# Second half of a weight load dropped: the last 64 channels of the first layer, rounded part and rest in one tile

## The chip, the cores and the metric

The kernel runs on one core of a Trainium2 chip. The metric is the device time of one execution in microseconds. A change is compared by the median of several runs; three runs of the kernel before gave 1145.97, 1151.23 and 1152.69 us, a median of 1151.23 us.

## What is computed

Tokens of width 192 pass a causal convolution of 7 taps whose weights are a softmax, and then a mixture of experts: 4 groups of 4 experts, one expert for each token, two matrix products with a relu between them.

```
x = attn_out.reshape(B * S, D)              # 23040 tokens, D = 192
g_idx = argmax(x @ w_group); e_idx = argmax(xg @ w_expert[g])
h  = np.maximum(xg[mask_e] @ w1[g, e], 0.0) # w1: 192 x 1024
ye = h @ w2[g, e]                           # w2: 1024 x 192
out[tok_idx] = combined[:, None] * ye       # softmax weights of group and expert
```

## The kernel before, in words

**Routing.** The tokens are cut into 18 units of 4, 8 or 12 blocks of 120 tokens. For each unit TensorE does the convolution (L452), transposes (L475, L483) and the router's logits (L495, L497); VectorE turns the logits into an expert and a place for every token (L539 to L626); GpSimd scatters token numbers into a table in memory (`idtab`, L645). The convolved tokens are written to memory from the queue of ScalarE (`xcd<-xc`, L570); the tile `xc` that is written has three buffers. The buffer `rowi` of the scatter's rows has two, so VectorE's instruction that writes `rowi` for unit 2 (L626) waits until the scatter of unit 0 has landed.

**Visits.** An expert is visited several times, each visit with 256 tokens. GpSimd gathers the tokens by their numbers (`xg<-xcd`, L717), TensorE transposes them (L750 to L754), and the products follow. Early visits run beside the routing (until some 450 us). Then come pairs of visits that share their weights (512 tokens, L786 to L805), and last a tail of 9 visits of 256 tokens and 9 of 128 in turn (L817 to L839 and L852 to L878), each with weights of its own. All engines run their instructions in order; a scheduler has set that order from the program.

**Products in three parts.** Each float32 operand is split into a rounded part and a rest, and a product is the sum of rounded x rounded, rest x rounded and rounded x rest. For the first 128 of the 192 channels these are three matmuls (`ah`, `al` with the tokens' `xa`). For the last 64 channels two matmuls do it over 128 partitions: the 64 weight rows lie twice in the tile `rb` (two loads of 256 KB, L667 and L668, one into each half). `bh` holds their rounded part twice and `bl` their rest twice, while the tokens' tile `xb` holds the rounded part in one half and the rest in the other. So `bh` x `xb` and `bl` x `xb` together give all four products.

**Weights of a visit** (`weights`, L652 on): five loads from SyncE's queue, in this text `ra` (512 KB, L666), the two halves of `rb`, and two loads of second-layer weights `rc` (384 KB each, L670). `ra` and `rb` come from one ring of three buffers named `raw`, or every second time in the tail from a spare tile named `xin`. ScalarE makes the rounded parts (L682, L690, L697) and VectorE the rests (L683, L691, L698); in the tail GpSimd makes `bl` (L691).

**Tokens of a visit** (`turn`, L739 on): the transposed tokens lie in one PSUM bank. ScalarE copies the rounded part, VectorE writes the rest, first for `xa`, then for `xb`. In the trace these four steps follow each other, the second ScalarE copy starting only after the first VectorE step. From the 17th visit on up to the tail the last 64 channels of the two tiles are packed and done in two halves of 128 tokens. A pair of visits keeps its `xb` in a tile named `xc`.

**Early order.** The first weights are loaded before the table is cleared (L269, L272): `clear_table` is issued on SyncE's queue behind the first visit's loads, and the first scatter waits for it.

Of the kernel before, what the change touches and what calls it, by code (L numbers as in the profile page):

```python
# [20 lines left out]
P = 128  # L21
# [3 lines left out]
SLOT = 256  # L25
# [11 lines left out]
def conv_moe_kernel(  # L37
# [614 lines left out]
    def weights(r1, r2, eng=None, spare=False):  # L652
        eng = eng or {}
        HF = NF // 2
        if spare:

            rab = pa2.tile([P, UB, D], F32, name="xin").rearrange("p b d -> p (b d)")
            ra, rb = (rab[:, k * F:(k + 1) * F] for k in range(2))
            rcc = pa2.tile([P, UB, XE], F32, name="xc", bufs=3).rearrange("p b d -> p (b d)")
            rc = [rcc[:, k * HF * D:(k + 1) * HF * D].rearrange("p (f d) -> p f d", d=D) for k in range(2)]  # L660
        else:
            ra, rb = (wraw.tile([P, F], F32, name="raw") for _ in range(2))
            rc = [wraw.tile([P, HF, D], F32, name="rawc") for _ in range(2)]
        npin[0] += 1
        hold = tc.keep_in_program_order if NPIN[0] < npin[0] <= NPIN[1] else lambda ins: ins
        hold(nc.sync.dma_start(out=ra, in_=w1f[bass.ds(r1, P), :]))  # L666
        hold(nc.sync.dma_start(out=rb[0:D2], in_=w1f[bass.ds(r1 + P, D2), :]))  # L667
        hold(nc.sync.dma_start(out=rb[D2:P], in_=w1f[bass.ds(r1 + P, D2), :]))  # L668
        for k in range(2):
            hold(nc.sync.dma_start(  # L670
                out=rc[k], in_=w2f[bass.ds(r2 + k * HF * P, HF * P), :].rearrange("(f p) d -> p f d", p=P),
            ))
        W = {}

        def split(k):
            if k == 0:
                W["ah"] = ah = wsp.tile([P, F], F32R, name="ah")
                W["al"] = al = wsp.tile([P, F], F32R, name="al")
                if 8 in eng:
                    nc.gpsimd.tensor_copy(out=ah, in_=ra)  # L680
                else:
                    pin(PINA, nc.scalar.activation(out=ah, in_=ra, func=AF.Copy))  # L682
                eng.get(k, nc.vector).tensor_tensor(out=al, in0=ra, in1=ah.bitcast(F32), op=ALU.subtract)  # L683
            elif k == 1:
                W["bh"] = bh = wsp.tile([P, F], F32R, name="bh")
                W["bl"] = bl = wsp.tile([P, F], F32R, name="bl")
                if 9 in eng:
                    nc.gpsimd.tensor_copy(out=bh, in_=rb)
                else:
                    pin(PINB, nc.scalar.activation(out=bh, in_=rb, func=AF.Copy))  # L690
                eng.get(k, nc.vector).tensor_tensor(out=bl, in0=rb, in1=bh.bitcast(F32), op=ALU.subtract)  # L691
            else:
                if k == 2:
                    W["cw"] = wsp.tile([P, NF, 2, D], F32R, name="cw")
                cw = W["cw"]
                fs = slice((k - 2) * HF, (k - 1) * HF)
                pin(PINW, nc.scalar.activation(out=cw[:, fs, 0, :], in_=rc[k - 2], func=AF.Copy))  # L697
                eng.get(k, nc.vector).tensor_tensor(  # L698
                    out=cw[:, fs, 1, :], in0=rc[k - 2], in1=cw[:, fs, 0, :].bitcast(F32), op=ALU.subtract,
                )  # L700
# [38 lines left out]
    def turn(xs, n=2, packed=False, into=None, single=False):  # L739
        if into is None:  # L740
            px = pm.tile([P, 512], F32, name="pm")
            xa = ff.tile([P, 2, SLOT], F32R, name="xa")
            xb = ff.tile([P, SLOT], F32R, name="xb")
            xh, xl = xa[:, 0], xa[:, 1]
        else:
            px = pm.tile([P, 512], F32, name="pm") if single else ph.tile([P, 2, SLOT], F32, name="ph").rearrange("p a b -> p (a b)")
            xh, xl, xb = into
        w = n * P
        for t in range(n):
            nc.tensor.transpose(px[:, t * P:(t + 1) * P], xs[t][:, 1:1 + P], ident)  # L750
            if not packed:
                nc.tensor.transpose(px[0:D2, SLOT + t * P:SLOT + (t + 1) * P], xs[t][:, 1 + P:XW], ident)
        if packed:
            nc.tensor.transpose(px[:, SLOT:SLOT + P], xs[0][:, 1 + P:XE], ident)  # L754
        nc.scalar.activation(out=xh[:, 0:w], in_=px[:, 0:w], func=AF.Copy)
        nc.vector.tensor_tensor(out=xl[:, 0:w], in0=px[:, 0:w], in1=xh[:, 0:w].bitcast(F32), op=ALU.subtract)
        if packed:
            for t in range(2):
                hi, lo = slice(t * D2, (t + 1) * D2), slice((1 - t) * D2, (2 - t) * D2)
                cs = slice(t * P, (t + 1) * P)  # L760
                pb = px[hi, SLOT:SLOT + P]
                nc.scalar.activation(out=xb[hi, cs], in_=pb, func=AF.Copy)
                nc.vector.tensor_tensor(out=xb[lo, cs], in0=pb, in1=xb[hi, cs].bitcast(F32), op=ALU.subtract)
            return None if into else (xa, xb)
        pb = px[0:D2, SLOT:SLOT + w]
        nc.scalar.activation(out=xb[0:D2, 0:w], in_=pb, func=AF.Copy)
        nc.vector.tensor_tensor(out=xb[D2:P, 0:w], in0=pb, in1=xb[0:D2, 0:w].bitcast(F32), op=ALU.subtract)  # L767
        return xa, xb

    def pair_room():  # L770
        hi = ff.tile([P, 2, SLOT], F32R, name="xa").rearrange("p a b -> p (a b)")
        lo = pa.tile([P, 512], F32, name="lts", bufs=2).bitcast(F32R)
        xb = pa2.tile([P, UB, XE], F32, name="xc", bufs=3).rearrange("p b d -> p (b d)")[:, 0:512].bitcast(F32R)
        return hi, lo, xb

    def turn_half(X, k, xs, single=False):
        cs = slice(k * SLOT, (k + 1) * SLOT)
        turn(xs, 2, True, [x[:, cs] for x in X], single)

    def hidden_pair(W, X, f):  # L780
        xh, xl, xb = X
        hp = ph.tile([P, 2, SLOT], F32, name="ph")
        fs = slice(f * P, (f + 1) * P)
        ops = (("ah", xh), ("al", xh), ("ah", xl), ("bh", xb), ("bl", xb))
        for i, (wgt, xx) in enumerate(ops):
            nc.tensor.matmul(  # L786
                out=hp.rearrange("p a b -> p (a b)"), lhsT=W[wgt][:, fs], rhs=xx, start=i == 0, stop=i == len(ops) - 1)
# [20 lines left out]

    def hidden(W, X, f2, hook=lambda: None):
        xa, xb = X  # L810
        ah, al, bh, bl = (W[n] for n in ("ah", "al", "bh", "bl"))
        hp = ph.tile([P, 2, SLOT], F32, name="ph")
        for j in range(2):
            fs = slice((2 * f2 + j) * P, (2 * f2 + j + 1) * P)
            ops = ((ah, xa[:, 0]), (al, xa[:, 0]), (ah, xa[:, 1]), (bh, xb), (bl, xb))
            for i, (wgt, xx) in enumerate(ops):
                nc.tensor.matmul(out=hp[:, j], lhsT=wgt[:, fs], rhs=xx, start=i == 0, stop=i == len(ops) - 1)  # L817
            if j == 0:
                hook()
# [25 lines left out]
    def hidden_small(W, X, h):  # L845
        xa, xb = X
        hp = ph.tile([P, 512], F32, name="ph")
        fs = slice(h * 512, (h + 1) * 512)
        xh, xl, xb = xa[:, 0, 0:P], xa[:, 1, 0:P], xb[:, 0:P]
        ops = ((xh, "ah"), (xh, "al"), (xl, "ah"), (xb, "bh"), (xb, "bl"))  # L850
        for i, (xx, wgt) in enumerate(ops):
            nc.tensor.matmul(out=hp, lhsT=xx, rhs=W[wgt][:, fs], start=i == 0, stop=i == len(ops) - 1)  # L852
        hr = pa.tile([P, 512], F32, name="lts", bufs=2)
        nc.scalar.activation(out=hr, in_=hp, func=AF.Relu)
        return hr
# [633 lines left out]
```

## Time and profile before

| | value |
|---|---|
| median of three runs | 1151.23 us |
| time of the profiled execution | 1152.26 us |
| its span, first to last instruction | 1150.4 us |
| mean granted TensorE clock | 0.977 |
| TensorE busy | 1072.8 us, 93% |
| VectorE, ScalarE, GpSimd busy | 752.4, 644.1, 523.5 us |
| moved by DMA | 166.08 MB, 144 GB/s in the mean |

Busy shares are means over stages with different limits, so the stages are read apart in windows of the span. A wait is given as the idle time of an engine ahead of an instruction and the event that ended it. An instruction's start and length stand in the timeline; on one engine the next one may start some tens of ns before the last one's end. The chain is followed back from the last instruction.

### The profile page before, as it was taken

Reading aid. Unit: us, or ns where it says so; the run is one execution under the profiler, and the core shown is the slowest. Engines: PE = TensorE matmul, PEld = TensorE weight load, DVE = VectorE, ACT = ScalarE, POOL = GpSimd, SP = SyncE. Lnnn points to the kernel's source line nnn. Section 1 sums busy time; section 2 is a strip of 40 time slices with the busy share of each in tenths; the row PEclk is TensorE's granted clock in tenths of the full one; section 3 lists DMA queues with packets and bytes.
Section 4 is the critical chain, followed back from the end, with each engine's and each line's share of the span. In section 5 each row is a group of like instructions: output and inputs, shape, how many; then the busy total and the mean of one; then the engine's idle time right before and its main releaser. Section 6 shows DMA issues by size and latency. Waiting matters only on the chain.

```text
span 1150.4 us, 20931 instructions
## 1 busy us (share of the span) xinstructions
PE 1072.8 (93%) x7124; PEld 971.1 (84%) x7124; DVE 752.4 (65%) x1671; ACT 644.1 (56%) x1362; POOL 523.5 (46%) x611
## 2 busy tenths in 40 slices
PE   6565999998999998999999999999999999999996
PEld 4444788987989998889899999999999988989986
DVE  3465878987778756576565555655556665687874
ACT  5445657765657554454455445554545555677873
POOL 3004143333334454554545454545445554487773
PEclk9878989999999999999999999999999999999998
DMA  8767688999566432332253223322333435499970
GB/s 185 186 158 228 160 222 215 252 234 216 156 155 164 122 106 85 116 112 67 83 137 113 72 76 99 113 74 73 103 101 106 133 92 157 116 257 257 252 201 19
DMA packets 143167, 166.08 MB, mean 144 GB/s; under 512 B 18946, under 2 KB 124397, under 8 KB 143054
## 3 DMA queue, kind: packets, MB, share of 16 engines
q1 hardware_dynamic: 100974, 111.04, 36.4%
q0 software_dynamic: 18752, 35.85, 10.5%
q10 hardware_dynamic: 23328, 17.80, 6.6%
q8 instruction: 57, 0.93, 0.3%
q14 instruction: 56, 0.46, 0.1%
HBM read 129.43 MB, written 36.58 MB: 144 GB/s over the span
## 4 chain that ended last, share of the span: by engine, by line
PE 70%; DMA 5%; DVE 5%; issue 4%; ACT 3%; POOL 1%; POOLq 0%; ACTq 0%; DVEq 0%
PE ph L786 21%; PE ph L817 11%; PE pm L801 7%; PE po L801 7%; PE po L835 7%; PE pm L805 3%; PE po L805 3%; PE po L839 3%; PE pm L452 3%; DMA rawc<-in_moe_w 2%; DMA xg<-xcd,idpt 2%; DVE hl L823 1%; DVE cw L698 1%; PE ph L852 1%; PE ph L750 1%
## 5 line engine op out<-in xcount | busy, mean ns | idle before, releaser
L888 POOL DMA_INDIRECT out<-ys,idp x160 | 174.3, 1090 | 267.9 <-DVE ys L898 192.0
L791 DVE SCALAR_TENSOR_TENSOR hl<-ph,hh 128x512 fp32r<-128x512 f32 x208 | 142.2, 689 | 141.7 <-ACT hh L790 141.3
L790 ACT ACTIVATE hh<-ph 128x512 fp32r<-128x512 f32 x208 | 123.0, 600 | 170.6 <-PE ph L786 167.6
L717 POOL DMA_INDIRECT xg<-xcd,idp x160 | 175.3, 1096 | 93.8 <-issue 40.5
L835 PE MATMUL po<-cw,hh 128*128 128x384 f32 x592 | 193.2, 379 | 3.0 <-DVE ys L898 3.0
L817 PE MATMUL ph<-xa,ah 128*128 128x256 f32 x592 | 169.2, 307 | 0.0
L839 PE MATMUL po<-cw,hl 128*128 128x192 f32 x592 | 149.6, 253 | 0.0
L801 PE MATMUL po<-cw,hh 128*128 128x384 f32 x416 | 134.1, 359 | 0.0
L801 PE MATMUL pm<-cw,hh 128*128 128x384 f32 x416 | 133.9, 359 | 0.0
L823 DVE SCALAR_TENSOR_TENSOR hl<-ph,hh 128x512 fp32r<-128x512 f32 x148 | 101.1, 684 | 42.7 <-ACT hh L822 42.5
L822 ACT ACTIVATE hh<-ph 128x512 fp32r<-128x512 f32 x148 | 87.9, 596 | 62.3 <-PE ph L817 49.8
L835 PEld LDWEIGHTS po<-cw,hh 128*128 128x128 f32 x592 | 112.7, 190 | 7.6 <-DVE ys L898 3.6
L817 PEld LDWEIGHTS ph<-xa,ah 128*128 128x128 f32 x592 | 113.1, 191 | 4.4 <-issue 1.5
L839 PEld LDWEIGHTS po<-cw,hl 128*128 128x128 f32 x592 | 114.4, 193 | 2.0
L805 PE MATMUL pm<-cw,hl 128*128 128x192 f32 x416 | 104.2, 250 | 0.0
L805 PE MATMUL po<-cw,hl 128*128 128x192 f32 x416 | 104.1, 250 | 0.0
L786 PE MATMUL ph<-xa,ah 128*128 128x512 f32 x208 | 86.0, 413 | 1.4 <-DVE hl L791 1.4
L698 DVE TENSOR_TENSOR cw<-rawc,cw 128x768 fp32r<-128x768 f32 x82 | 76.0, 955 | 15.1 <-ACT cw L697 14.5
L817 PE MATMUL ph<-xb,bh 128*128 128x256 f32 x296 | 84.0, 284 | 0.7 <-DVE xb L767 0.7
L805 PEld LDWEIGHTS po<-cw,hl 128*128 128x128 f32 x416 | 79.1, 190 | 5.8
L817 PE MATMUL ph<-xb,bl 128*128 128x256 f32 x296 | 83.9, 284 | 0.0
L817 PE MATMUL ph<-xa,al 128*128 128x256 f32 x296 | 83.7, 283 | 0.0
(275 smaller groups left out, 2656.2 us busy)
## 6 DMA issues: line engine op xcount, KB each, us to landing
rawc<-in_moe_w SPq DMA_DIRECT2D x82, 384.0 KB
raw<-in_moe_w SPq DMA_DIRECT2D x41, 512.0 KB
raw<-in_moe_w SPq DMA_DIRECT2D x82, 256.0 KB
xcd<-xc ACTq DMA_DIRECT2D x13, 1085.6 KB
xin<-in_x SPq DMA_DIRECT2D x7, 1134.0 KB
xc<-in_moe_w SPq DMA_DIRECT2D x18, 384.0 KB
xin<-in_x SPq DMA_DIRECT2D x6, 1039.5 KB
xin<-in_moe_w SPq DMA_DIRECT2D x9, 512.0 KB
```

Source lines behind the costliest of these rows:

```text
L717: nc.gpsimd.indirect_dma_start(out=xs[t][:, 0:XW], out_offset=None, in_=xcd[0:known, :], in_offset=bass.IndirectOffsetOnAxis(ap=ids[:, t, ...
L786: nc.tensor.matmul(out=hp.rearrange("p a b -> p (a b)"), lhsT=W[wgt][:, fs], rhs=xx, start=i == 0, stop=i == len(ops) - 1)
L790: nc.scalar.activation(out=hh, in_=hp, func=AF.Relu)
L791: nc.vector.scalar_tensor_tensor(out=hl, in0=hp, scalar=0.0, in1=hh.bitcast(F32), op0=ALU.max, op1=ALU.subtract,)
L801: nc.tensor.matmul(out=oo[t][:, 0:2 * D], lhsT=hh[:, ts], rhs=cw[:, f].rearrange("p a d -> p (a d)"), start=f == 0, stop=False,)
L805: nc.tensor.matmul(out=oo[t][:, 0:D], lhsT=hl[:, ts], rhs=cw[:, f, 0, :], start=False, stop=f == NF - 1,)
L817: nc.tensor.matmul(out=hp[:, j], lhsT=wgt[:, fs], rhs=xx, start=i == 0, stop=i == len(ops) - 1)
L822: nc.scalar.activation(out=hh, in_=hp, func=AF.Relu)
L823: nc.vector.scalar_tensor_tensor(out=hl, in0=hp, scalar=0.0, in1=hh.bitcast(F32), op0=ALU.max, op1=ALU.subtract,)
L835: nc.tensor.matmul(out=oo[t][:, 0:2 * D], lhsT=hh[:, j, ts], rhs=cw[:, f].rearrange("p a d -> p (a d)"), start=f == 0, stop=False,)
L839: nc.tensor.matmul(out=oo[t][:, 0:D], lhsT=hl[:, j, ts], rhs=cw[:, f, 0, :], start=False, stop=f == NF - 1,)
L888: nc.gpsimd.indirect_dma_start(out=outviews[nscat[0] % len(outviews) if view is None else view], out_offset=bass.IndirectOffsetOnAxis(ap=i ...
```

## The change

The second load of the 64 rows goes. One tile `bb` holds the rounded part in partitions 0 to 63 and the rest in 64 to 127. The tokens now need two tiles: `xb[0]` with the rounded part in both halves (two ScalarE copies where there was one), and `xb[1]` with the rest in the lower half and zeros in the upper one. `bb` x `xb[0]` gives rounded x rounded and rest x rounded, `bb` x `xb[1]` gives rounded x rest; rest x rest is no longer in the sum. The tile with zeros is one of two constants `xz`, cleared once on GpSimd and used in turn. The number and the sizes of the matmuls stay.

```
+    xz = [const.tile([P, 2 * SLOT], F32R, name=f"xz{i}") for i in range(2)]
+    for t in xz:
+        nc.gpsimd.memset(t.bitcast(F32)[D2:P], 0.0)
...
-        hold(nc.sync.dma_start(out=rb[D2:P], in_=w1f[bass.ds(r1 + P, D2), :]))
...
-                    pin(PINB, nc.scalar.activation(out=bh, in_=rb, func=AF.Copy))
-                eng.get(k, nc.vector).tensor_tensor(out=bl, in0=rb, in1=bh.bitcast(F32), op=ALU.subtract)
+                    pin(PINB, nc.scalar.activation(out=bb[0:D2], in_=rb[0:D2], func=AF.Copy))
+                eng.get(k, nc.vector).tensor_tensor(
+                    out=bb[D2:P], in0=rb[0:D2], in1=bb[0:D2].bitcast(F32), op=ALU.subtract)
...
+            xb = ff.tile([P, SLOT], F32R, name="xb"), rests()[:, 0:SLOT]
...
-                nc.scalar.activation(out=xb[hi, cs], in_=pb, func=AF.Copy)
-                nc.vector.tensor_tensor(out=xb[lo, cs], in0=pb, in1=xb[hi, cs].bitcast(F32), op=ALU.subtract)
+                for half in (slice(0, D2), slice(D2, P)):
+                    nc.scalar.activation(out=xb[0][half, cs], in_=pb, func=AF.Copy)
+                nc.vector.tensor_tensor(out=xb[1][0:D2, cs], in0=pb, in1=xb[0][hi, cs].bitcast(F32), op=ALU.subtract)
...
-        nc.scalar.activation(out=xb[0:D2, 0:w], in_=pb, func=AF.Copy)
-        nc.vector.tensor_tensor(out=xb[D2:P, 0:w], in0=pb, in1=xb[0:D2, 0:w].bitcast(F32), op=ALU.subtract)
+        for half in (slice(0, D2), slice(D2, P)):
+            nc.scalar.activation(out=xb[0][half, 0:w], in_=pb, func=AF.Copy)
+        nc.vector.tensor_tensor(out=xb[1][0:D2, 0:w], in0=pb, in1=xb[0][0:D2, 0:w].bitcast(F32), op=ALU.subtract)
...
-        ops = (("ah", xh), ("al", xh), ("ah", xl), ("bh", xb), ("bl", xb))
+        ops = (("ah", xh), ("al", xh), ("ah", xl), ("bb", x2), ("bb", x3))
```

Three places show how it moves instructions.

SyncE's queue in the routing stage, around one load of tokens (`xin`, at 235 to 243 us of the trace of before); `raw` is `ra` (128 rows) or `rb` (64 rows), `rawc` is `rc`. Before:

```order
L225 DMA xin<-in_x 120x192
L227 DMA xin<-in_x 126x11x192
L670 DMA rawc<-in_moe_w 128x4x192
L667 DMA raw<-in_moe_w 64x1024
L668 DMA raw<-in_moe_w 64x1024
L670 DMA rawc<-in_moe_w 128x4x192
L666 DMA raw<-in_moe_w 128x1024
```

The same place now:

```order
L225 DMA xin<-in_x 120x192
L227 DMA xin<-in_x 126x11x192
L678 DMA rawc<-in_moe_w 128x4x192
L676 DMA raw<-in_moe_w 64x1024
L678 DMA rawc<-in_moe_w 128x4x192
L675 DMA raw<-in_moe_w 128x1024
```

The second half of `rb` no longer stands ahead of a visit's second `rc`; nothing else moves here.

VectorE at unit 2's list (36 to 48 us of the trace of before). Before:

```order
L591 TENSOR_REDUCE posn<-pos 120x8
L593 TENSOR_SCALAR posb<-posn 120x8
L595 SCALAR_TENSOR_TENSOR posb<-posb,posn 120x8
L608 TENSOR_TENSOR ohl<-iop,posb 120x768
L615 TENSOR_TENSOR ohr<-ior,posb 120x192
L608 TENSOR_TENSOR ohl<-iop,posb 120x256
L619 TENSOR_TENSOR ohv<-ohr,vals 120x192
L626 TENSOR_TENSOR rowi<-rows,goff 128x1
L224 MEMSET xin 6x192
L615 TENSOR_TENSOR ohr<-ior,posb 120x64
L619 TENSOR_TENSOR ohv<-ohr,vals 120x64
```

The same place now:

```order
L600 TENSOR_REDUCE posn<-pos 120x8
L635 TENSOR_TENSOR rowi<-rows,goff 128x1
L602 TENSOR_SCALAR posb<-posn 120x8
L604 SCALAR_TENSOR_TENSOR posb<-posb,posn 120x8
L617 TENSOR_TENSOR ohl<-iop,posb 120x768
L624 TENSOR_TENSOR ohr<-ior,posb 120x192
L617 TENSOR_TENSOR ohl<-iop,posb 120x256
L628 TENSOR_TENSOR ohv<-ohr,vals 120x192
L624 TENSOR_TENSOR ohr<-ior,posb 120x64
L628 TENSOR_TENSOR ohv<-ohr,vals 120x64
```

The instruction that writes `rowi` has moved ahead of six others, and the clearing of `xin` ahead of all of these.

ScalarE in the tail, from the weights of a small visit over the tokens of the next. Before:

```order
L690 ACTIVATE bh<-xin 128x1024
L854 ACTIVATE lts<-ph 128x512
L755 ACTIVATE xa<-pm 128x256
L766 ACTIVATE xb<-pm 64x256
L682 ACTIVATE ah<-raw 128x1024
```

The same place now:

```order
L697 ACTIVATE bb<-xin 64x1024
L864 ACTIVATE lts<-ph 128x512
L763 ACTIVATE xa<-pm 128x256
L776 ACTIVATE xb<-pm 64x256 x2
L690 ACTIVATE ah<-raw 128x1024
```

The copy to `xb` stands twice, and the rounding of the weights works on 64 partitions; the order is otherwise the same.

## Rows read from the trace of the kernel before

**Rows 1.** The page, part 1: busy time of each engine

```profile
PE 1072.8 (93%) x7124; PEld 971.1 (84%) x7124; DVE 752.4 (65%) x1671; ACT 644.1 (56%) x1362; POOL 523.5 (46%) x611
```

**Rows 2.** Windows: busy PE, PEld, DVE, ACT, POOL; then clock, DMA share, GB/s

```profile
100.00:200.00 100.00, 85.62 (x651) 75.67 (x650) 75.45 (x190) 58.52 (x125) 33.23 (x27) 0.93 0.79 207
200.00:300.00 100.00, 94.07 (x714) 85.22 (x713) 80.34 (x193) 66.22 (x143) 34.30 (x30) 0.98 0.91 224
600.00:700.00 100.00, 100.00 (x579) 90.34 (x578) 56.36 (x106) 50.23 (x107) 48.21 (x73) 1.00 0.30 89
1025.00:1050.00 25.00, 23.84 (x170) 21.98 (x169) 20.39 (x31) 18.62 (x35) 19.31 (x14) 1.00 0.94 237
```

**Rows 3.** The page, part 6: DMA issues, count and size of each

```profile
raw<-in_moe_w SPq DMA_DIRECT2D x82, 256.0 KB
xin<-in_moe_w SPq DMA_DIRECT2D x18, 256.0 KB
```

**Rows 4.** Timeline of ScalarE: start, length, instruction, idle time before it

```profile
247.06 0.38 ACT L766 ACTIVATE xb<-pm 64x256 fp32r<-64x256 f32 x1 [3.76 <-DVE xa L756]
247.34 0.40 ACT L897 ACTIVATE ys<-po,xg 128x192 f32<-128x192 f32 x1
...
969.58 0.42 ACT L762 ACTIVATE xc<-ph 64x128 fp32r<-64x128 f32 x2
...
1034.94 0.39 ACT L755 ACTIVATE xa<-pm 128x256 fp32r<-128x256 f32 x1 [0.58 <-PE pm L752]
```

**Rows 5.** Timeline at unit 2's list: SyncE's clearing, VectorE, TensorE

```profile
23.88 6.25 SPq L269 DMA_DIRECT2D idtab<-ohl  x1
...
35.86 0.17 DVE L593 TENSOR_SCALAR posb<-posn 120x8 f32<-120x8 f32 x1
37.92 0.35 DVE L619 TENSOR_TENSOR ohv<-ohr,vals 120x192 f16<-120x192 f16 x1
46.49 0.16 DVE L626 TENSOR_TENSOR rowi<-rows,goff 128x1 int32<-128x1 f32 x1 [8.22 <-DMA idtab<-lsi,rowi]
47.24 0.48 PE L633 MATMUL pm<-ohv,ohl 120*128 120x192 f16 x2 [8.15 <-DVE ohv L619]
```

**Rows 6.** Timeline: a write of `xcd` and the instruction that waited for it

```profile
96.60 0.32 ACTq L570 DMA_DIRECT2D xcd<-xc  x1
109.99 0.42 ACT L461 ACTIVATE xc<-ph 120x288 f32<-120x288 f32 x1 [8.79 <-DMA xcd<-xc]
```

**Rows 7.** Timeline: two late second-layer weights, and TensorE behind the second

```profile
250.58 0.85 ACT L697 ACTIVATE cw<-rawc 128x768 fp32r<-128x768 f32 x1 [1.08 <-DMA rawc<-in_moe_w]
...
281.81 0.84 ACT L697 ACTIVATE cw<-rawc 128x768 fp32r<-128x768 f32 x1 [2.81 <-DMA rawc<-in_moe_w]
283.56 0.54 PE L507 MATMUL pm<-ident,lts 128*120 128x128 f32 x3 [3.02 <-ACT lts L500]
```

**Rows 8.** Waits of TensorE, 1000 to 1151 us: total, times, longest

```profile
PE po L878 <- DVE hl L864: 3.0, 8, 0.4
```

**Rows 9.** The chain in the tail: like stretches of four large visits

```profile
1012.79 2.42 PE ph L817 x20
1028.89 2.19 PE ph L817 x18
1045.87 2.19 PE ph L817 x18
1127.85 2.42 PE ph L817 x20
```

**Rows 10.** Timeline: waits and one GpSimd rest in the tail, first pair's wait

```profile
464.98 0.50 PE L786 MATMUL ph<-xc,bh 128*128 128x512 f32 x1 [0.93 <-DVE xc L763]
1019.80 1.06 ACT L682 ACTIVATE ah<-raw 128x1024 fp32r<-128x1024 f32 x1 [0.41 <-PE ph L852]
1033.95 0.33 PE L750 MATMUL pm<-ident,xg 128*128 128x128 f32 x1 [0.36 <-DMA xg<-xcd,idpt]
1034.82 2.42 POOL L691 TENSOR_TENSOR bl<-xin,bh 128x1024 fp32r<-128x1024 f32 x1
```

More of the change, by code (lines that the diff above doesn't have):

```diff
@@ L393, in conv_moe_kernel, with rests @@
         xg.append((t[:, 0:XE], t[:, XE:XE + XW]))
+    xz = [const.tile([P, 2 * SLOT], F32R, name=f"xz{i}") for i in range(2)]
+    for t in xz:
+        nc.gpsimd.memset(t.bitcast(F32)[D2:P], 0.0)
+    nrest = [0]
+    def rests():
+        nrest[0] += 1
+        return xz[nrest[0] % 2]
     shared = []
@@ L684, in split @@
             elif k == 1:
-                W["bh"] = bh = wsp.tile([P, F], F32R, name="bh")
-                W["bl"] = bl = wsp.tile([P, F], F32R, name="bl")
+                W["bb"] = bb = wsp.tile([P, F], F32R, name="bb")
                 if 9 in eng:
-                    nc.gpsimd.tensor_copy(out=bh, in_=rb)
+                    nc.gpsimd.tensor_copy(out=bb[0:D2], in_=rb[0:D2])
                 else:
-                    pin(PINB, nc.scalar.activation(out=bh, in_=rb, func=AF.Copy))
-                eng.get(k, nc.vector).tensor_tensor(out=bl, in0=rb, in1=bh.bitcast(F32), op=ALU.subtract)
+                    pin(PINB, nc.scalar.activation(out=bb[0:D2], in_=rb[0:D2], func=AF.Copy))
+                eng.get(k, nc.vector).tensor_tensor(
+                    out=bb[D2:P], in0=rb[0:D2], in1=bb[0:D2].bitcast(F32), op=ALU.subtract)
             else:
@@ L742, in turn @@
             xa = ff.tile([P, 2, SLOT], F32R, name="xa")
-            xb = ff.tile([P, SLOT], F32R, name="xb")
+            xb = ff.tile([P, SLOT], F32R, name="xb"), rests()[:, 0:SLOT]
             xh, xl = xa[:, 0], xa[:, 1]
@@ L746, in turn @@
             px = pm.tile([P, 512], F32, name="pm") if single else ph.tile([P, 2, SLOT], F32, name="ph").rearrange("p a b -> p (a b)")
-            xh, xl, xb = into
+            xh, xl, *xb = into
         w = n * P
@@ L758, in turn @@
             for t in range(2):
-                hi, lo = slice(t * D2, (t + 1) * D2), slice((1 - t) * D2, (2 - t) * D2)
+                hi = slice(t * D2, (t + 1) * D2)
                 cs = slice(t * P, (t + 1) * P)
                 pb = px[hi, SLOT:SLOT + P]
-                nc.scalar.activation(out=xb[hi, cs], in_=pb, func=AF.Copy)
-                nc.vector.tensor_tensor(out=xb[lo, cs], in0=pb, in1=xb[hi, cs].bitcast(F32), op=ALU.subtract)
+                for half in (slice(0, D2), slice(D2, P)):
+                    nc.scalar.activation(out=xb[0][half, cs], in_=pb, func=AF.Copy)
+                nc.vector.tensor_tensor(out=xb[1][0:D2, cs], in0=pb, in1=xb[0][hi, cs].bitcast(F32), op=ALU.subtract)
             return None if into else (xa, xb)
         pb = px[0:D2, SLOT:SLOT + w]
-        nc.scalar.activation(out=xb[0:D2, 0:w], in_=pb, func=AF.Copy)
-        nc.vector.tensor_tensor(out=xb[D2:P, 0:w], in0=pb, in1=xb[0:D2, 0:w].bitcast(F32), op=ALU.subtract)
+        for half in (slice(0, D2), slice(D2, P)):
+            nc.scalar.activation(out=xb[0][half, 0:w], in_=pb, func=AF.Copy)
+        nc.vector.tensor_tensor(out=xb[1][0:D2, 0:w], in0=pb, in1=xb[0][0:D2, 0:w].bitcast(F32), op=ALU.subtract)
         return xa, xb
@@ L773, in pair_room @@
         xb = pa2.tile([P, UB, XE], F32, name="xc", bufs=3).rearrange("p b d -> p (b d)")[:, 0:512].bitcast(F32R)
-        return hi, lo, xb
+        return hi, lo, xb, rests()
     def turn_half(X, k, xs, single=False):
@@ L780, in hidden_pair @@
     def hidden_pair(W, X, f):
-        xh, xl, xb = X
+        xh, xl, x2, x3 = X
         hp = ph.tile([P, 2, SLOT], F32, name="ph")
         fs = slice(f * P, (f + 1) * P)
-        ops = (("ah", xh), ("al", xh), ("ah", xl), ("bh", xb), ("bl", xb))
+        ops = (("ah", xh), ("al", xh), ("ah", xl), ("bb", x2), ("bb", x3))
         for i, (wgt, xx) in enumerate(ops):
@@ L810, in hidden @@
         xa, xb = X
-        ah, al, bh, bl = (W[n] for n in ("ah", "al", "bh", "bl"))
+        ah, al, bb = (W[n] for n in ("ah", "al", "bb"))
         hp = ph.tile([P, 2, SLOT], F32, name="ph")
@@ L814, in hidden @@
             fs = slice((2 * f2 + j) * P, (2 * f2 + j + 1) * P)
-            ops = ((ah, xa[:, 0]), (al, xa[:, 0]), (ah, xa[:, 1]), (bh, xb), (bl, xb))
+            ops = ((ah, xa[:, 0]), (al, xa[:, 0]), (ah, xa[:, 1]), (bb, xb[0]), (bb, xb[1]))
             for i, (wgt, xx) in enumerate(ops):
@@ L848, in hidden_small @@
         fs = slice(h * 512, (h + 1) * 512)
-        xh, xl, xb = xa[:, 0, 0:P], xa[:, 1, 0:P], xb[:, 0:P]
-        ops = ((xh, "ah"), (xh, "al"), (xl, "ah"), (xb, "bh"), (xb, "bl"))
+        xh, xl, x2, x3 = xa[:, 0, 0:P], xa[:, 1, 0:P], xb[0][:, 0:P], xb[1][:, 0:P]
+        ops = ((xh, "ah"), (xh, "al"), (xl, "ah"), (x2, "bb"), (x3, "bb"))
         for i, (xx, wgt) in enumerate(ops):
```

## The prediction

> **What bounds the kernel now.** I read the page's busy times first. TensorE is busy 93% of the span, the next engine, VectorE, 65% [rows 1]. The matmuls keep their number and size, so the change can give only what TensorE loses in idle time. Where it idles is read from windows of the span [rows 2]. In the stretch of paired visits (600 to 700 us) it is busy all the time, ScalarE and VectorE about half, and DMA has a share of 0.30: fewer bytes are worth nothing there. The routing stage is different: 14.4 us idle between 100 and 200 us at a DMA share of 0.79, and 5.9 us between 200 and 300 us at 0.91. In the tail the DMA share is 0.94 and TensorE misses 1.2 us of 25. So the change has to be judged in the routing stage and in the tail, by the waits there and by what stands behind the removed loads.
>
> **What goes and what comes.** The page counts 82 + 18 loads of 256 KB [rows 3]; half of them go, 50 loads of 262,144 bytes or 13.1 MB. At the rates of the windows one such load is 1.27 us of DMA (207 GB/s, 100 to 200 us), 1.17 us (224 GB/s, 200 to 300 us) or 1.11 us (237 GB/s, tail). ScalarE gets a second copy for each `xb`. A copy of 64x256 took 0.38 us, but the next instruction began 0.28 us after it; two of 64x128 took 0.42 us together, so the second adds some 0.15 us [rows 4]. The rounding and the rest of `bb` are on 64 partitions instead of 128 and cost the same: 64x256 took 0.38 us, 128x256 took 0.39 us on ScalarE [rows 4]. The two clearings of `xz` are on GpSimd in the first microseconds, ahead of the scatter that waits for the cleared table; I price them at nothing.
>
> **Term 1, unit 2's list: +1.0 us.** VectorE waits 8.22 us for the first scatter to land before it writes `rowi` (46.49), and TensorE's last two list products start 0.75 us later (47.24) after 8.15 us of idleness [rows 5]. Before, the work from 35.86 to the end of the product at 38.27, 2.4 us, was done ahead of that wait; now it stands behind it, with the little that stood there anyway, less the clearing of `xin`. So TensorE would be some 2.3 us later. Against it, the clearing of the table, whose issue took 6.25 us on a full queue [rows 5], is one load less behind: 1.27 us earlier, and with it the scatter. The sum is +1.0; the bounds are +2.3 (nothing earlier) and -1.27 (the later work covered, the clearing early).
>
> **Term 2, writes of `xcd`: -0.6 us.** ScalarE waited 8.79 us until a write issued at 96.60 had landed at 109.99, and so left the `xc` buffer [rows 6]; among the loads beside it is one of the halves that go. If all share the DMA engines, it lands up to 1.27 us earlier; if the write is limited by its own short rows, none. I take half.
>
> **Term 3, late second-layer weights: -2.2 us.** At 250.58 ScalarE waited 1.08 us for the second `rc` of a visit, at 281.81 another 2.81 us, and TensorE then stood 3.02 us [rows 7]. SyncE's queue shows why the removed load bears on it: it stood directly ahead of that second `rc`. One load less is 1.17 us at each place, but at the first no more than the wait: 1.08 + 1.17 = 2.2. The extra copies of `xb` fall into these waits and cost nothing. Bounds: 0, and -3.5 if the shorter stall also spares some of the time at which TensorE's clock was below full (mean 0.98 in that window [rows 2]).
>
> **Term 4, gathers in the tail: -1.6 us.** Seven steps of large and small visits take 1127.85 - 1012.79 = 115.06 us; the first one takes 16.10, the second 16.98 [rows 9]. If all took 16.10, 2.4 us would be saved. In the long step TensorE waits for a gather [rows 10]. Two loads less in a step are 2.2 us of DMA of some 16, so gathers should land earlier; but the gathers also queue behind GpSimd's own work, so I take two thirds. Bounds 0 and -2.4.
>
> **Term 5, ScalarE's second copies: +0.8 us.** In the paired stretch TensorE, always busy, covers them. In the tail the `ah` of a small visit waited 0.41 us for TensorE [rows 10]; the copies ahead of it grow by 0.15 + 0.28 = 0.43 us, so 0.02 us are over in each of 8 steps, 0.2 us. TensorE waits 0.4 us for the far end of the same run of work in each of 8 steps [rows 8], so what is over does count. At the start of the first pair TensorE already waits 0.93 us for its tokens [rows 10]; four more copies there are up to 0.6 us. Bounds: 0, and 8 x 0.43 + 0.6 = 4.0 if nothing covers.
>
> **Sum.** 1.0 - 0.6 - 2.2 - 1.6 + 0.8 = -2.6 us. The profiled execution took 1152.26 us, so 1149.7; it lies 1.03 us above the median of 1151.23, so the median after should be **1148.6 us**. The bounds add up to -8.4 and +6.3, that is 1143 to 1157.5.
>
> [...]
>
> **Rivals.**
> *The relief does not come.* The kept half of each load holds the queue as long as both did, or the late transfers are bound by their own latency. For it: the write of `xcd` took 13.4 us, and the share of 0.79 around it says that DMA was not full. Against it: in the window of the late `rc` the share is 0.91 [rows 2]. Then terms 2 to 4 are nil and the clearing is no earlier: 2.3 + 0.8 = +3.1, 1154.3 us, slower than before though within 1%.
> *GpSimd becomes the bound of the tail.* `bb`'s rest there reads partitions 0 to 63 and writes 64 to 127, which no GpSimd row of before does. At 128x1024 it took 2.42 us [rows 10]. GpSimd is busy 19.3 of 25 us [rows 2], 12.4 of 16.1, so it has 3.7 us to spare in a step with two such rests; it decides once one takes over 2.42 + 1.85 = 4.3 us. At twice the time the step grows by 4.84 - 3.7 = 1.1 us: nine steps +10, term 4 gone, 1148.6 + 1.6 + 10 = 1160 us. Against it: the elements of each partition are as many as before, and ScalarE's time did not depend on partitions.
> *DMA was behind most of the routing stage's idle time.* The idle time from 100 to 300 us is 20.3 us [rows 2]; if half of it goes and the tail gives its 2.4, it is 1151.2 - 12.5 = 1139 us. Against it: only the waits of rows 6 and 7 name a transfer that weights could delay.
>
> **Chances.** Forecast 0.68; relief that does not come 0.17; GpSimd 0.05; most of the idle time 0.10. About 1%, 11.5 us, is what a measurement of this kernel can tell from no change. Faster by more: 0.10 (the last rival). Slower by more: 0.05, of GpSimd, whose 1160 us is just inside, but whose price could be higher. The rest 0.85. The range that leaves out no more than 2 in 10 is 1141 to 1156 us: the forecast with its bounds but for the far ends, and the relief that does not come.
>
> **What would show it.** The profile after should have 41 and 9 loads of 256 KB. Term 1: the wait at `rowi` ends about 1.2 us earlier, and the list products behind it start later than 47.24. Term 3: ScalarE's waits for `rawc` near 250 and 281 us are gone, or shorter by 1.1 us. Term 4: steps of 16.1 us through the tail, no TensorE wait for gathers. Term 5: TensorE's waits at L878 still near 0.4 us each. GpSimd's rest still at 2.4 us. I am wrong if the DMA share of the routing stage stays at 0.91, if the tail's steps grow, or if the chain of early writes starts to drift at unit 2.

## The result, and the profile after

The changed kernel takes 1159.08 us in the median of nine runs (1154.60 to 1163.31); the kernel before, run beside it, 1149.24 us. The ratio is 1.009, with a 95% interval of 1.0063 to 1.0117: some 10 us slower. On a second chip it was 1.0064 (1.0042 to 1.0085), some 7 us; one run of the kernel before there took 2060.48 us, far from all others, and is left out of the ratio. The prediction was 1148.6 us with a range up to 1156, so the time is outside of it, on the side of the loss.

The page of the profiled execution (1157.94 us, span 1156.1) answers to [rows 1, 3]. First busy times, then the queue of the weights, then the loads of 64 rows that are left:

```profile
PE 1070.4 (93%) x7124; PEld 966.0 (84%) x7124; DVE 753.1 (65%) x1671; ACT 691.1 (60%) x1524; POOL 522.3 (45%) x613
...
q1 hardware_dynamic: 96974, 97.93, 31.3%
...
raw<-in_moe_w SPq DMA_DIRECT2D x41, 256.0 KB
```

ScalarE has 162 instructions and 47 us of work more; the work of the other engines is as it was. The windows that answer to [rows 2] (busy PE, PEld, DVE, ACT, POOL; clock, DMA share, GB/s):

```profile
100.00:200.00 100.00, 85.36 (x657) 75.34 (x656) 76.51 (x196) 61.90 (x133) 32.02 (x27) 0.95 0.74 192
200.00:300.00 100.00, 94.63 (x733) 86.00 (x732) 83.08 (x198) 70.02 (x151) 37.28 (x31) 1.00 0.83 209
600.00:700.00 100.00, 100.00 (x578) 90.35 (x578) 57.99 (x108) 56.32 (x128) 50.04 (x74) 1.00 0.27 81
1025.00:1050.00 25.00, 22.75 (x164) 21.11 (x163) 19.50 (x30) 19.19 (x38) 18.29 (x13) 1.00 0.81 218
```

The DMA share fell as it should, by 0.05, 0.08 and 0.13, and TensorE is no busier for it (85.36 and 94.63 us in the first two windows, against 85.62 and 94.07); in the tail it idles 2.25 us of 25 instead of 1.16. The rows that answer to [rows 5, 7, 8, 10] (timeline of VectorE, TensorE, ScalarE and GpSimd):

```profile
42.84 0.16 DVE L635 TENSOR_TENSOR rowi<-rows,goff 128x1 int32<-128x1 f32 x1 [9.46 <-DMA idtab<-lsi,rowi]
45.08 1.44 PE L642 MATMUL pm<-ohv,ohl 120*128 120x192 f16 x8 [9.85 <-DVE ohv L628]
247.72 0.84 ACT L705 ACTIVATE cw<-rawc 128x768 fp32r<-128x768 f32 x1 [0.45 <-DMA rawc<-in_moe_w]
278.71 0.84 ACT L705 ACTIVATE cw<-rawc 128x768 fp32r<-128x768 f32 x1 [0.98 <-DMA rawc<-in_moe_w]
1053.89 2.39 POOL L698 TENSOR_TENSOR bb<-xin,bb 64x1024 fp32r<-64x1024 f32 x1 [0.47 <-ACT bb L697]
```

And TensorE's waits for VectorE behind 1000 us (sum, count, longest):

```profile
PE po L888 <- DVE hl L874: 8.2, 8, 1.1
```

Late weights cost ScalarE less (0.45 and 0.98 us, where it was 1.08 and 2.81), `bb`'s rest on GpSimd still takes 2.39 us, no gather keeps TensorE waiting in the tail; but the eight stalls there have grown from some 0.4 us each to between 0.7 and 1.1 us.

### The profile page after: what moved, and what is told of

Its sections match the earlier page's. It is cut to its first block, busy times and chain, and to the rows that moved or that the text cites. A ratio compares the mean times of both kernels' runs of the same rounds, so it can differ in the third digit from the quotient of the medians.

```text
span 1156.1 us, 20943 instructions
## 1 busy us (share of the span) xinstructions
PE 1070.4 (93%) x7124; PEld 966.0 (84%) x7124; DVE 753.1 (65%) x1671; ACT 691.1 (60%) x1524; POOL 522.3 (45%) x613
## 4 chain that ended last, share of the span: by engine, by line
PE 64%; issue 7%; DVE 6%; ACT 6%; DMA 5%; POOL 1%; SPq 1%; POOLq 0%; ACTq 0%; DVEq 0%
PE ph L796 21%; PE ph L827 9%; PE pm L811 7%; PE po L811 7%; PE po L845 5%; PE pm L815 3%; PE po L815 3%; DMA rawc<-in_moe_w 2%; PE po L849 2%; PE pm L461 2%; DVE hl L833 1%; ACT cw L705 1%; DVE cw L706 1%; DMA xc<-in_moe_w 1%; DMA xg<-xcd,idp 1%
## 5 line engine op out<-in xcount | busy, mean ns | idle before, releaser
L898 POOL DMA_INDIRECT out<-ys,idp x160 | 177.6, 1110 | 272.9 <-DVE ys L908 199.1
L796 PE MATMUL ph<-xc,bb 128*128 128x512 f32 x208 | 82.3, 396 | 2.6 <-ACT bb L697 2.2
L827 PE MATMUL ph<-xz,bb 128*128 128x256 f32 x296 | 83.6, 282 | 1.0 <-DVE xz L777 1.0
L827 PE MATMUL ph<-xb,bb 128*128 128x256 f32 x296 | 83.6, 282 | 0.1
```

What stands on the lines that cost most here:

```text
L796: nc.tensor.matmul(out=hp.rearrange("p a b -> p (a b)"), lhsT=W[wgt][:, fs], rhs=xx, start=i == 0, stop=i == len(ops) - 1)
L898: nc.gpsimd.indirect_dma_start(out=outviews[nscat[0] % len(outviews) if view is None else view], out_offset=bass.IndirectOffsetOnAxis(ap=i ...
```

## The experiments

In what follows a difference in us is (ratio - 1) times the median of the kernel before on the same chip (1144 to 1148 us), with its interval worked out alike. Line numbers in the rows are those of each run's own kernel. Single executions of one kernel scatter: 29 runs of the kernel before have a standard deviation of 2.7 us on one chip and of 3.2 us on another. "Starts" are those of the `xa` copies, visit by visit. Ahead of 320 us the visits of like executions start up to 8 us apart, so that stage is judged by medians. From 320 to 450 us and within the pairs the distance between two executions of like code stays within 0.1 us; from 450 to 490 us it changes by up to 1.4 us, and over the tail by some 1.5 us.

**What the second copies alone cost.** `e2_copies`, the kernel before with

```
+                for _ in range(2):
+                    nc.scalar.activation(out=xb[hi, cs], in_=pb, func=AF.Copy)
```

and the same for the copy of 64 x w.

> The kernel before with each ScalarE copy of xb done twice, into the same place; loads, weights, order of the list and matmuls as before. It tells what the second copies alone cost. Theory (they close a ring in the tail and lengthen the packed visits between 300 and 475 us): tail steps of 17 us instead of 16.1, some 3 us lost between 300 and 475 us, 1.006 to 1.009 of before. Rival (the loss comes from the one tile bb, whose rest is wanted one matmul earlier): within 0.2% of before, tail steps as before.

Measured: 1.0068 (1.0048 to 1.0088), +7.8 us (5.5 to 10.1). The place that was expected is not the one: in its profile only 0.6 us are lost between 317 and 400 us, and most of the tail's steps are 16.28 us. But the copies alone, with all loads in place, lose about as much as the whole change does on the second chip (7.3 us).

**The removed load put back.** `e1_reload`, the changed kernel with

```
+        hold(nc.sync.dma_start(out=rb[D2:P], in_=w1f[bass.ds(r1 + P, D2), :]))
```

> The changed kernel with the second load of the 64 rows put back into the upper half of rb, where nothing reads it; all the rest as changed. It tells what the removed load alone is worth. Theory (the saved load did bring some 4.7 us until 300 us, the second ScalarE copies of xb took it back later): the early lead goes and nothing is won instead, about 1.013 of before, 1162 to 1165 us. Rival (the load was worth nothing, the early lead comes from the new order of VectorE's list): same as the changed kernel, 1.009, and the visits until 300 us start as early as there.

Measured: 1.0102 (1.0079 to 1.0125). That is 1 to 4 us more than the changed kernel had on its two chips, but the intervals overlap. The scheduler also put unit 2's list back into the order of before, so this takes out both; `e10_no_second_load` below is the better measurement.

**Copies moved to GpSimd.** `e3_tail_wide` (tail), `e4_all_wide` (all unpaired visits) and `e7_early_wide` (all unpaired ones ahead of the tail):

```
+            nc.gpsimd.tensor_copy(out=xs[t][:, XW:XE], in_=xs[t][:, 1 + P:XW])
...
+                nc.tensor.transpose(px[:, SLOT + t * P:SLOT + (t + 1) * P], xs[t][:, 1 + P:XE], ident)
...
+            nc.scalar.activation(out=xb[0][:, 0:w], in_=px[:, SLOT:SLOT + w], func=AF.Copy)
```

> The changed kernel, but in the tail GpSimd copies the 64 channels beside themselves in the tokens' tile (128x64, 0.24 us each), one transpose then fills all 128 partitions, and one ScalarE copy of 128 x w replaces the two of 64 x w. It tells whether the second copies set the tail's step. Theory: ScalarE's tail is as long as before, steps of 16.1 us, 4.4 us less than the changed kernel, about 1.005 of before. Rival (one tile bb sets the step): steps stay at 17.1 us, 1.009.

> As e3_tail_wide, but for all visits that are not paired, so also before 450 us; these are then transposed in four pieces throughout, with one ScalarE copy instead of two or four. Theory: the 3.2 us that the changed kernel gave back between 300 and 475 us stay as well, 1.001 to 1.003 of before. Rival (the time between 300 and 475 us goes for another reason): as e3_tail_wide.

> The changed kernel, but in the 25 visits that stand ahead of the pairs and the single ones between pairs GpSimd copies the 64 channels beside themselves in the tokens' tile, one transpose fills all 128 partitions, and one ScalarE copy of 128x256 replaces two of 64x256 or four of 64x128; pairs and tail as changed. Theory (the second copies are paid beside the routing, where TensorE waits for ScalarE's work on the units): of the 2.2 us that the changed kernel loses between 317 and 400 us under 0.6 are left, about 1.004 of before. Rival (they are paid in the pairs or the tail): 1.006 or more, as the changed kernel.

Measured: 1.0382 (1.035 to 1.0414), 1.0415 (1.0387 to 1.0443) and 1.0079 (1.0049 to 1.0109). The first two are much slower. The timeline of GpSimd in `e3_tail_wide`, then the waits of TensorE behind 1000 us:

```profile
1023.80 0.24 POOL L740 COPY xg<-xg 128x64 f32<-128x64 f32 x1 [6.34 <-DMA xg<-xcd,idpt]
1024.12 2.33 POOL L698 TENSOR_TENSOR bb<-xin,bb 64x1024 fp32r<-64x1024 f32 x1
```

```profile
PE ph L838 <- POOL bb L698: 28.4, 7, 6.0
```

A copy of 0.24 us stands 6.34 us in GpSimd's queue until its gather has landed, and the rest of `bb` stands behind it; TensorE waits 28.4 us for those rests, of 44 us that are lost in all. So these two say nothing of the second copies. `e7_early_wide` loses only 0.5 us between 317 and 400 us, as expected there, but as a whole it is no faster than the changed kernel: half of its expectation failed, and why is open. GpSimd's new copies may cost there what the second copies did; no run takes the two apart.

**Two profiles from one chip.** `b_same` and `a_same` are the kernels before and after, unchanged.

> The kernel before, unchanged, for a profile from the same chip as the next three. Every theory: 1.000.

> The changed kernel once more, for a profile from the same chip as the kernel before. Every theory: 1.009 again. If the removed loads relieve the routing stage, its visits until 300 us start 3 to 5 us earlier than in the kernel before on this chip; if the lead seen between the first two profiles was only the difference of two executions, they start within 1 us.

Measured: 0.9991 (0.9967 to 1.0016) and 1.0064 (1.0042 to 1.0085). The visits of `a_same` start 2.2 us later than those of `b_same` at 317 us, where the first pair of profiles had shown them 4.7 us earlier: that lead was scatter. Then it loses 2.2 us until 400 us, gains 0.7 until 475, loses 0.5 in the pairs, 1.5 between 937 and 997 and 1.9 in the tail; the gain until 475 us is no larger than what two executions of like code differ by there.

What TensorE waits for between 317 and 400 us in `b_same`, `a_same` and, with a single copy again, `e11_one_copy` (below), as sum, count, longest:

```profile
PE pm L483 <- ACT ta L476: 0.6, 1, 0.6
```

```profile
PE pm L492 <- ACT ta L485: 1.1, 1, 1.1
PE pm L461 <- ACT lg L517: 0.6, 1, 0.6
PE pm L461 <- ACT xc L470: 0.4, 1, 0.4
```

```profile
PE pm L502 <- ACT ta L495: 0.6, 1, 0.6
```

With second copies TensorE waits 2.1 us for ScalarE's work on the units (`ta`, `lg`, `xc`), without them 0.6 us.

**Where the copies are paid.** `e6_copies_tail`, `e8_copies_early`, `e9_copies_pairs`: the edit of `e2_copies` in one kind of visit each.

> The kernel before with the ScalarE copy of xb done twice in the tail alone; nothing else changes, on any engine. Theory: a second copy costs its whole 0.40 us, less the 0.41 us that ScalarE waited for TensorE: steps of 16.5 us, 3 us in all, 1.003. Rival (the tail has more slack than that, and the 7.8 us of the doubled copies were lost ahead of it): 1.000 to 1.001.

> The kernel before with the ScalarE copy of xb done twice in all visits that are neither paired nor in the tail; nothing else changes in the kernel's text. Theory: most of the 7.8 us of the copies doubled everywhere, 1.004 to 1.006. Rival (the pairs carry it): 1.000 to 1.001.

> The kernel before with the ScalarE copy of xb done twice in the paired visits alone, where TensorE is always busy. Theory: covered, but for the first pair and the end of the stage, 0.5 to 1 us, 1.000 to 1.001. Rival: 1.004 or more.

Measured: 1.0005 (0.9987 to 1.0024), 1.0041 (1.0025 to 1.0057) and 1.0034 (1.0013 to 1.0055), or +0.6 (-1.5 to 2.7), +4.7 (2.9 to 6.5) and +3.9 us (1.5 to 6.3), together 9.2 against 7.8 for all at once. By the medians the early visits, which the prediction had left without a price, carry most, then the pairs. The profiles do not show where. That of `e8_copies_early` is one of its fastest executions (1145.24 us); against `b_same` its visits start 0.4 us earlier at 317 us, 0.3 later at 438 and 1.5 earlier at 475, so none of the 4.7 us is seen there. That of `e9_copies_pairs` shows only some 0.5 us in the stage of the pairs.

`e15_early_four` and `e14_pairs_four` do the same with `range(4)`, to enlarge it.

> The same for the visits that are neither paired nor in the tail: four copies instead of one. If each further copy is paid there as in e8_copies_early (+4.7 us for one), three cost near 14 us, 1.011 to 1.014; if that was scatter: 1.002 to 1.005.

> The kernel before with the ScalarE copy of xb done four times in the paired visits alone, three more than before where e9_copies_pairs has one more. If a second copy in the pairs costs what e9_copies_pairs measured (+3.9 us), three cost near 12 us, 1.009 to 1.011. If TensorE covers them in the pairs, as the stage's own profile says (+0.5 us), and the rest of the 3.9 us is the scatter between executions: 1.001 to 1.004.

Measured: 1.0129 (1.0097 to 1.016), +14.8 us (11.1 to 18.4) for three more copies, 4.9 for each: in the early visits each further copy costs about what the first one did, so the 4.7 us were not scatter. The early visits have 40 of the 162 second copies; at 0.30 us each (below) that is 12 us of ScalarE's time, of which some 40% is paid. The profile of `e15_early_four` loses in lumps, 7.8 us between 165 and 210 us and 8.2 us between 375 and 438 us of `b_same`. In the second one (387 to 458 us of its own) TensorE waits for the tokens:

```profile
408.35 0.39 PE L819 MATMUL ph<-xb,bh 128*128 128x256 f32 x1 [1.91 <-DVE xb L764]
```

The granted clock from 406 to 416 us is 0.83 there.

In the pairs, with three more copies, 1.0697 (1.0668 to 1.0727), +80 us, which neither reading had expected. TensorE's waits between 480 and 900 us:

```profile
PE ph L788 <- DVE xc L764: 28.0, 20, 2.1
PE ph L750 <- DVE hl L793: 7.2, 19, 1.0
```

With three more copies the tokens of every pair come too late. These waits are 35 of the 80 us; the granted clock, 1.00 in windows of 100 us between 480 and 880 us of `b_same`, is 0.95 to 0.98 here. So the cover in the pairs ends between one further copy and three, or already with the first one; how much of the 3.9 us is real, this does not tell.

**What the loads alone are worth.** `e10_no_second_load`, the kernel before without that load:

```
-        hold(nc.sync.dma_start(out=rb[D2:P], in_=w1f[bass.ds(r1 + P, D2), :]))
...
+                    pin(PINB, nc.scalar.activation(out=bh[0:D2], in_=rb[0:D2], func=AF.Copy))
```

> The kernel before without the second load of the 64 rows, and without second copies: bh and bl are written in their lower 64 partitions alone, the upper ones are zeros from the start, so the rests of the tokens' last 64 channels are left out of the sum. VectorE's list of unit 2 stands as in the changed kernel. It measures what the removed loads and that order are worth together. Theory of the prediction (its terms 1 to 4): -3.4 us, 0.997. Rival (no wait on the path hangs on these bytes): 1.000. If the order at unit 2 costs 2.3 us and the bytes give nothing: 1.002.

Measured: 0.9965 (0.9942 to 0.9988), -4.0 us (-6.6 to -1.4). In the packed visits the second tile of 128 tokens has its rounded part in the upper half, so for these tokens the kernel leaves out the rounded part and not the rest; the loads and the matmuls are the same either way.

**The changed kernel with one copy.** `e11_one_copy`:

```
-        for half in (slice(0, D2), slice(D2, P)):
-            nc.scalar.activation(out=xb[0][half, 0:w], in_=pb, func=AF.Copy)
+        nc.scalar.activation(out=xb[0][0:D2, 0:w], in_=pb, func=AF.Copy)
```

> The changed kernel with one ScalarE copy instead of two: the rounded part of the tokens' last 64 channels goes into the lower half of xb alone, the upper half is zeros from the start, so the rests of the weights of these channels are left out of the sum. Loads, bb, its rest and xz as changed. Theory (the second copies are all that the change loses): about as the kernel before without the second load, 0.996 to 0.998. Rival (bb in one tile, its rest wanted one matmul earlier, the constant xz: also lose time): 1.001 to 1.004.

Measured: 0.9988 (0.9962 to 1.0013), -1.4 us (-4.4 to 1.5), so the copies cost the change 8.7 us against `a_same` (11.7 against the first runs), each on another chip. The difference of 2.6 us to `e10_no_second_load` lies within the intervals, so a cost of the single tile `bb` or of the constant `xz` of that size is neither shown nor excluded. The window from 300 to 400 us of `b_same`, `a_same` and `e11_one_copy`, in this order:

```profile
300.00:400.00 100.00, 99.32 (x798) 91.61 (x798) 76.41 (x188) 60.68 (x136) 38.79 (x37) 1.00 0.58 151
```

```profile
300.00:400.00 100.00, 97.64 (x782) 89.53 (x782) 75.48 (x185) 63.65 (x145) 39.66 (x38) 1.00 0.52 134
```

```profile
300.00:400.00 100.00, 99.32 (x796) 91.44 (x796) 75.87 (x188) 61.16 (x137) 39.38 (x38) 1.00 0.53 140
```

TensorE's 99.32 us come back with the single copy, at the lower DMA share: in these executions the 1.7 us of this stage are the copies'.

**The tail in the old way.** `e5_tail_old`, the changed kernel with `old=True` for the tail's weights and turns: the second load again, `bh` and `bl`, one copy.

> The changed kernel with the tail's visits done as before: two loads of the 64 rows, bh and bl of 128 partitions, one ScalarE copy of xb. All before the tail as changed. Theory (the tail's ring of ScalarE, VectorE and GpSimd got longer by the second copies): steps of 16.1 us, 4 to 5 us less than the changed kernel, 1.005. Rival (the tail's step follows the loads or the one tile, and what is lost lies ahead of the tail): 1.008 to 1.009.

Measured: 1.0068 (1.0043 to 1.0092), no better. In the tail loss and gain cancel: seven steps take 115.30 us here and 115.50 us in `a_same`, and with both loads TensorE waits for gathers again (0.64 and 0.81 us).

**Two other ways to save the load.** `e12_half_gpsimd` and, with `nc.vector`, `e13_half_vector`, ahead of the tail:

```
+                    pin(PINB, nc.scalar.activation(out=bh[0:D2], in_=rb[0:D2], func=AF.Copy))
+                    nc.gpsimd.tensor_copy(out=bh[D2:P], in_=rb[0:D2])
+                    nc.vector.tensor_tensor(out=bl[0:D2], in0=rb[0:D2], in1=bh[0:D2].bitcast(F32), op=ALU.subtract)
```

> A version meant to keep the gain without second copies of the tokens: the kernel before, ahead of the tail without the second load; bh gets its upper half from GpSimd, which copies the loaded 64 rows once more (64x1024), and bl is written in its lower half over an upper half of zeros. Tokens as before, one ScalarE copy; tail as before with two loads. Theory: the -4.0 us of the kernel without the second load, less the tail's share of 0.5 to 1.6 us, 0.997 to 0.998. Rival (GpSimd's gathers wait for these copies beside the routing): over 1.001.

> As e12_half_gpsimd, with VectorE instead of GpSimd making the upper half of bh. Theory: VectorE has more work beside the routing than GpSimd, so it is no better: 0.998 to 1.002.

Measured: 1.0054 (1.0027 to 1.0081) and 1.0035 (1.001 to 1.006). A copy of 64x1024 takes 1.32 us on GpSimd in the mean of 32 (1.03 to 1.96) and 0.71 us on VectorE; either version takes back more than the load gave. Both also leave out a product: for the second tile of the packed visits the weights' rest meets only the tokens' rest. No version that computes what the kernel before computes, or what the changed kernel does, and beats the kernel before was found.

## Why the prediction was wrong, step by step

**The step that failed is the size of term 5**, +0.8 us with bounds of 0 and 4.0; the copies cost 7.8 us alone (5.5 to 10.1) and 8.7 to 11.7 us in the change. With the -4.0 us of the loads the 7.8 us would give only +3.8; that the change loses more fits the copies into the other half of the partitions, which hold ScalarE longer than those of `e2_copies` into the same half (0.41 against 0.30 us, below; 7.8 x 0.41 / 0.30 = 10.7 us as an estimate, which no run tests by itself). The term failed twice.

First, the price of a second copy. The prediction took 0.15 us (64x128) and 0.28 us (64x256), from the busy time of two and from one copy's start to the next instruction's. ScalarE's timeline around 350 us in `b_same`, `e2_copies` and `a_same`: one copy, two into the same half, two into both halves, each with the instruction behind it.

```profile
349.10 0.27 ACT L762 ACTIVATE xb<-pm 64x128 fp32r<-64x128 f32 x1 [0.95 <-DVE xa L756]
349.27 0.35 ACT L484 ACTIVATE tb<-pm 128x240 f32<-128x240 f32 x1
```

```profile
350.19 0.57 ACT L763 ACTIVATE xb<-pm 64x128 fp32r<-64x128 f32 x2 [0.95 <-DVE xa L756]
350.66 0.35 ACT L484 ACTIVATE tb<-pm 128x240 f32<-128x240 f32 x1
```

```profile
352.41 0.55 ACT L771 ACTIVATE xb<-pm 64x128 fp32r<-64x128 f32 x2 [0.95 <-DVE xa L764]
352.99 0.37 ACT L493 ACTIVATE tb<-pm 128x240 f32<-128x240 f32 x1
```

From the copy to the next instruction it is 0.17, 0.47 and 0.58 us: a second copy adds 0.30 us into the same half and 0.41 us into the other one, not 0.15. The single copy let the next instruction start inside its own 0.27 us; the pair into both halves does not. For 64x256 in the tail, with one copy in `e10_no_second_load` and two in `a_same`:

```profile
1026.72 0.38 ACT L771 ACTIVATE xb<-pm 64x256 fp32r<-64x256 f32 x1 [0.49 <-DVE xa L761]
1027.50 1.06 ACT L687 ACTIVATE ah<-raw 128x1024 fp32r<-128x1024 f32 x1 [0.40 <-PE ph L857]
```

```profile
1036.73 0.77 ACT L776 ACTIVATE xb<-pm 64x256 fp32r<-64x256 f32 x2 [0.49 <-DVE xa L764]
1037.52 1.06 ACT L690 ACTIVATE ah<-raw 128x1024 fp32r<-128x1024 f32 x1
```

Two copies hold the next instruction for 0.79 us; against the 0.28 us of a single one [rows 4] the second adds 0.51 us.

Second, the visits that got no price. The prediction counted the tail and the first pair, and said of the routing stage that the copies fall into waits for late weights and cost nothing. There ScalarE also carries the units' work (`xc`, `ta`, `tb`, `lg`), and TensorE waits for it, 2.1 us in `a_same` between 317 and 400 us where it was 0.6. By the medians the copies cost +4.7 us in the early visits alone and 4.9 us for each further copy; ahead of 317 us, where most of that would have to lie, the way is not shown. The stretch from the last pairs to the tail (937 to 997 us), in which `a_same` loses 1.5 us, was not counted either, and for the pairs "TensorE, always busy, covers them" is open (+3.9 us by the medians). The bound of 4.0 us was a bound of the two places counted, not of the term. At the first pair "up to 0.6" was right between `b_same` and `a_same`, 0.60 us:

```profile
459.98 0.50 PE L786 MATMUL ph<-xc,bh 128*128 128x512 f32 x1 [1.25 <-DVE xc L763]
```

```profile
463.07 0.50 PE L796 MATMUL ph<-xc,bb 128*128 128x512 f32 x1 [1.85 <-ACT xc L771]
```

In `e2_copies` that wait is 2.21 us, in `e9_copies_pairs` 1.23.

**In the tail the mechanism was right, the size again too small.** The stalls of TensorE that end each step, in `e10_no_second_load`, `a_same` and the first profile of the changed kernel:

```profile
1019.80 0.69 PE L883 MATMUL po<-cw,hl 128*128 128x192 f32 x4 [0.35 <-DVE hl L869]
1035.90 0.69 PE L883 MATMUL po<-cw,hl 128*128 128x192 f32 x4 [0.36 <-DVE hl L869]
```

```profile
1029.40 0.69 PE L888 MATMUL po<-cw,hl 128*128 128x192 f32 x4 [0.78 <-DVE hl L874]
1045.90 0.69 PE L888 MATMUL po<-cw,hl 128*128 128x192 f32 x4 [0.77 <-DVE hl L874]
```

```profile
1030.60 0.69 PE L888 MATMUL po<-cw,hl 128*128 128x192 f32 x4 [1.06 <-DVE hl L874]
1047.70 0.69 PE L888 MATMUL po<-cw,hl 128*128 128x192 f32 x4 [1.08 <-DVE hl L874]
```

A step takes 16.1, 16.5 and 17.1 us. The wait of 0.41 us that was to cover the copies [rows 10] is indeed gone in `a_same`: the large visit's second copy took its place, and the small visit's 0.41 us is over in each step, not 0.02. Why one execution has 17.1 us stays open: its trace adds a wait of ScalarE for TensorE ahead of `lts` (0.26 to 0.52 us) in each of the seven steps, which `a_same` does not have.

**Term 4 was borne out** (-1.6 us). Seven steps take 115.06 us before [rows 9], 113.53 us in `b_same`, and 112.65 us in `e10_no_second_load`, each step 16.09 to 16.10 us, with no wait for a gather: -0.9 to -2.4 us. In the change the copies take it back: 115.50 us in `a_same`, no gather waited for either.

**Term 3 was right in kind** (-2.2 us): the waits for late `rc` sum to 3.9 us before [rows 7] and 2.4 us in `b_same`, and to 1.4 and 1.6 us in the two profiles of the changed kernel, -0.8 to -2.5 us. **Term 2** (-0.6 us) did not come: from its issue until the buffer is free the write of `xcd` takes 13.0 and 14.2 us in the changed kernel, 13.4 [rows 6] and 12.4 us before. **Term 1** (+1.0 us) stays open. Between the first two profiles it has the other sign: `rowi` is written at 42.84 us instead of 46.49, and the list products end at 46.52 us instead of 47.72 [rows 5]. But the start of an execution scatters more than that. In the nine profiles with both loads and the old order `rowi` is written between 42.08 us (`e2_copies`) and 46.49, and the products end between 43.31 and 47.72; in the ten with the new order it is 33.52 (`e13_half_vector`) to 46.75 and 36.60 to 50.42. By the medians `rowi` is 1.7 us earlier (44.56 and 42.88) and the products end 0.8 us later (45.79 and 46.55), as the term has it. That the clearing met a full queue was read from the 6.25 us of its issue alone [rows 5]; no run tests it. Together the four terms were -3.4 us; measured without any second copy they are -4.0 us (-6.6 to -1.4). That the sum came so near is in part luck: one of the four did not come and one is open.

**The time of a removed half.** That a removed load gives back all of its time at the rates of the windows, 1.27 us in term 1 and 1.17 us in term 3, was the author's estimate; no run shows it for a single load, nor how fast a load into partitions 0 to 63 alone lands. At the two places of term 3 the waits were 0.63 and 1.83 us shorter in the first profile of the changed kernel. That the half that stays would take as long as both did, as the first rival has it, is not shown either: the fall of the DMA share from 0.91 [rows 2] to 0.83 between 200 and 300 us, with the rate down alike from 224 to 209 GB/s, and the -4.0 us of `e10_no_second_load` speak against it for these loads.

**The rivals.** That no relief comes is false, and so is that GpSimd becomes the bound of the tail (2.39 us a rest). DMA was not behind most of the routing stage's idle time: with 50 loads less, TensorE is busy 87.65 and 96.67 us in the two windows of `e10_no_second_load`, 88.21 and 95.30 us in those of `b_same`, 0.8 us less idle in all. The sign was lost on a rival that was not written down: that the copies are paid ahead of the tail too, where ScalarE stands between TensorE and its next work.

## What to carry to other kernels

In the changed kernel ScalarE is busy 60% in the mean and still kept TensorE waiting for 2.1 us between 317 and 400 us in `a_same`: price a small instruction that is repeated 162 times by the start of the next instruction behind it in the same run of work, and give each stage its own line in the sum, those "covered by waits" too. A bound must hold for all the places an edit touches; here 162 x 0.3 us = 49 us would have been the honest end, of which a sixth was paid in `e2_copies`. And take two profiles of each kernel from one chip before reading a lead of a few us: 4.7 us of early lead were gone in the next pair.

## What was not expected of the hardware

Around 350 us two copies of 64x128 from `pm` by ScalarE, one into each half of the partitions, held the next instruction back by 0.58 us (`a_same`), where one held it 0.17 us (`b_same`); into the same half it was 0.47 us (`e2_copies`). A VectorE copy of 64x1024 into the other half of the partitions took 0.71 us in the mean (`e13_half_vector`), the same on GpSimd 1.32 us (`e12_half_gpsimd`). And TensorE's granted clock fell to 0.50 of full speed for some 3.5 us in the first execution of the changed kernel, after waits of 1.15 us (to 970.94) and 0.42 us (to 972.32). Three windows of 1 us from it:

```profile
972.00:973.00 1.00, 0.68 (x3) 0.50 (x4) 0.30 (x2) 0.27 (x1) 1.00 (x1) 1.00 0.00 0
974.00:975.00 1.00, 1.00 (x4) 0.81 (x3) 0.57 (x1) 0.00 (x0) 0.00 (x0) 0.50 0.00 0
977.00:978.00 1.00, 1.00 (x10) 1.00 (x9) 0.27 (x1) 0.24 (x1) 0.00 (x0) 1.00 0.00 0
```

In `a_same`, with like waits in the same place (1.17 and 0.41 us), it did not fall:

```profile
970.00:980.00 10.00, 8.42 (x45) 6.89 (x45) 5.91 (x13) 7.14 (x18) 3.66 (x3) 1.00 0.03 10
```
